# Chunked attention with a channel mix on one core: q and k of the first tiles loaded two tokens a partition, with a reordered start

## The chip, the cores and the metric

The kernel runs on one core of a Trainium2 chip. The metric is the device time of one execution in microseconds, as the median of several runs. The engines are TensorE (PE, with its weight loads PEld), VectorE (DVE), ScalarE (ACT), GpSimd (POOL) and SyncE (SP). SP issues nearly all DMAs, in the order in which the program names them; each engine works off its own instructions in order.

## The reference

q, k and v are (8, 8, 576, 64): batch, heads, tokens, head dimension, float32. The weights of the channel mix come in float64 and are read as words.

```python
# attention inside chunks of 64 tokens
scores = scale * q_c @ k_c^T          # per batch, head, chunk: 64 x 64
attn = softmax(scores)                # max subtracted, 1e-9 added to the sum
x = heads side by side of attn @ v_c  # (8, 576, 512)
# channel mix
x_prev = x shifted by one token, zero at the start of a batch
xk = mu_k * x + (1 - mu_k) * x_prev
xr = mu_r * x + (1 - mu_r) * x_prev
k = relu(xk @ w_k)                    # 512 -> 1024
v = (k * k) @ w_v                     # 1024 -> 512
out = sigmoid(xr @ w_r) * v
```

## The kernel before

The 8 x 576 = 4608 tokens are cut into 36 tiles of 128 tokens, two to a group of 256 (18 groups). A tile holds two chunks of 64 tokens. Its work is named by tasks:

- **n, b, v, s** are loads on SP: `nq`/`nk` q and k in natural layout (tokens on partitions) for the first six tiles, `bq`/`bk` 32 x 32 blocks of q and k for the later groups, `v`, and `swr`, `swk`, `swv` the staged pieces of 1 MB of the weights (two of w_r, four of w_k, four of w_v).
- **T** brings q and k into the layout with the head dimension on partitions (`qT`, `kT`, one buffer each): for the first six tiles by PE transposes (line 318) and copies out of PSUM (133), later by DVE's block transpose (339).
- **S** are the scores (363) and the softmax: maximum (373), subtraction (379), exp on ACT (383), sums (387 to 389), normalization (393). **P** transposes the probabilities (420), multiplies by v (438) and writes x.
- **Mk, Mr** are the two token mixes. For tiles 0 to 3 PE makes them by products with diagonal matrices of mu and 1 - mu (528); later tiles use DVE, with a difference d (510) and four operations of 128 columns (540). Each mix is split into a high and a low part, in the format of the fast products.
- **c, h** turn a staged float64 piece into a high and a low part, with two ACT operations (258, 262), two DVE operations (265, 271), a copy (133) on either engine and a subtraction on DVE (280).
- **K, R, V** are the products with w_k (580), w_r (629) and w_v (659), each in three passes of high and low parts. **K** is followed by relu (594), square (601) and the split (133, 613), **R** by the sigmoid (643), **V** by the product with it and the store (672, 674).

A staged w_k piece lies in a slot of a later w_v tile, the w_r pieces and the first two w_v pieces in rings of the K results, and the last two w_v pieces in one ring called `st`, of one buffer. The diagonals lie in that ring too (line 481). `d` and `mix` tiles have two buffers each.

The order of all instructions is written by hand. `START` lists every step of the first groups, with the engine behind a colon (A for ACT, D for DVE), as in

```python
W:14 Mk3.0:D nq0.0 nk0.0 T0.2 T0.0 T0.3:D mu.0:A T0.1:D Mk0.0:D nq1.0 P0.3:D nk1.0 T1.0 S0.0
```

`T0.2` is the third step of task T0, `W:14` fourteen warm-up products. `GROUP` lists the steps of one pass of the loop for groups 2 to 17, which computes K, R and V of its group, attention and mixes of the next, and the loads of the ones behind. Semaphores between the engines follow from the tiles that the steps read and write.

Of the kernel before, what the change touches and what calls it, by code (L numbers as in the profile page):

```python
# [7 lines left out]
F32 = mybir.dt.float32  # L8
# [3 lines left out]
AF = mybir.ActivationFunctionType  # L12
ALU = mybir.AluOpType
# [11 lines left out]


START = """
W:14 Mk3.0:D nq0.0 nk0.0 T0.2 T0.0 T0.3:D mu.0:A T0.1:D Mk0.0:D nq1.0 P0.3:D nk1.0 T1.0 S0.0
S0.1:D swr0.0 dg.0:A v0.0 S0.2:D nk2.0 S0.3:A T1.1:D T1.2 T1.3:A cwr0.0:A S1.0 nk3.0 cwr0.1:A
S0.4:D S0.5:D S1.1:D T2.2 S1.2:D T2.3:A nq2.0 cwr0.2:D P0.0 cwr0.3:D P0.1:A P0.2 swr1.0 S1.3:A  # L30
T3.2 P0.4:A nq3.0 S1.4:D S1.5:D hwr0.0:A cwr1.0:D Mr0.0 cwr1.1:A v1.0 T2.0 P1.0 swk0.0 hwr0.1:D
nq4.0 T2.1:A P1.1:A P1.3:D cwr1.2:D Mk0.1 nk4.0 T3.3:A cwr1.3:D Mr0.1:A S2.0 T3.0 S2.1:D P1.2
Mk0.2:A Mr0.2:D nq5.0 T3.1:A S2.2:D S3.0 P1.4:A nk5.0 T4.2 swk1.0 S3.1:D cwk0.1:A Mk0.3:D
cwk0.0:A S3.2:D S2.3:A T4.0 T4.3:A Mk1.1 hwr1.0:A v2.0 Mr1.0 swk3.0 T4.1:A Mk1.2:A T5.2 Mr1.1:A
S2.4:D S2.5:D T5.3:A hwr1.1:D Mk1.3:D S3.3:A swk2.0 cwk0.2:D cwk0.3:D cwk1.1:A Mr1.2:D P2.0
P2.1:A hwk0.0:A S3.4:D T5.0 S3.5:D P2.3:D Mk2.0:D Mk1.0:D hwk0.1:D R00.0 P2.2 R00.1:A R01.0
P2.4:A cwk2.1:A cwk1.0:D cwk1.2:D T5.1:A P3.0 cwk1.3:D P3.1:A cwk2.0:A Mr2.0 Mr2.1:A K00.0
hwk1.0:D v3.0 hwk1.1:D cwk2.2:D R01.1:A P3.2 cwk2.3:D cwk3.0:A S4.0 K01.0 S5.0 swv1.0 P3.3:D
Mk2.1 swv0.0 cwk3.1:A hwk2.0:A cwk3.2:D hwk2.1:D cwk3.3:D K00.1:A K01.1:A K02.0 K00.2:A
hwk3.0:D cwv0.0:A K01.2:A hwk3.1:D bq3.0 cwv0.1:A Mr2.2:D K03.0 P3.4:A cwv1.0:A Mk2.2:A  # L40
cwv0.2:D P4.3:D cwv0.3:D Mk3.1 Mk2.3:D v4.0 cwv1.1:A Mr3.0 swv2.0 Mk3.2:D Mk3.3:D S4.1:D
K00.3:A Mr3.1:A K00.4:D hwv0.0:A Mr3.2:D K02.1:A R10.0 K10.0 K01.3:A T6.0:D K02.2:A cwv1.2:D
K02.3:A K01.4:D cwv1.3:D R11.0 R10.1:A K03.1:A cwv2.0:A cwv2.1:A K11.0 hwv0.1:D K03.2:A K02.4:D
R11.1:A K03.3:A S5.1:D cwv2.2:D V001.0 cwv2.3:D K10.1:A K03.4:D hwv2.0:A hwv1.0:A S4.2:D S4.3:A
hwv2.1:D K12.0 V001.1 v5.0 hwv1.1:D V001.2 K10.2:A S5.2:D S4.4:D S5.3:A bk3.0 K11.1:A K11.2:A
K10.3:A S4.5:D S5.4:D K10.4:D swv3.0 P4.0 P4.1:A K11.3:A S5.5:D cwv3.1:A V001.3 P4.2 cwv3.0:D
K11.4:D K12.1:A K13.0 K12.2:A bq4.0 P4.4:A V001.4 cwv3.2:D cwv3.3:D hwv3.0:A P5.3:D P5.0 V001.5
T7.0:D P5.1:A K13.1:A hwv3.1:D V001.6 Mk4.0:D K12.3:A V001.7 Mk4.1:D V001.8:D Mk4.2:A P5.2 v6.0
V10.0 P5.4:A V001.9:D V10.1 V11.0 Mk5.0:D Mr4.0:D V11.1 K13.2:A K13.3:A Mr4.1:A Mk4.3:D K12.4:D
Mk5.1:D V10.2 V10.3 Mk5.2:A K13.4:D V11.2 V11.3 V10.4 Mr4.2:D Mk5.3:D V11.4 V10.5 V11.5 v7.0  # L50
T6.1:D V10.6 Mr5.0:D Mr5.1:D V10.7 V11.6 Mr5.2:D V11.7 bk4.0 T7.1:D V11.8:D V10.8:D
"""
# [26 lines left out]
def tile_chunk_attention_channel_mix(  # L79
# [57 lines left out]
    def queue(e):  # L137
        return nc.scalar if e == "A" else nc.sync
# [7 lines left out]
    def segments(first, many):  # L146

        cut = -first % S
        if 0 < cut < many:
            return [(0, cut), (cut, many - cut)]  # L150
        return [(0, many)]

    def load_nat(t):
        for nm, src in (("q", q), ("k", k)):
            do.task = f"n{nm}{t}"

            def fn(_, nm=nm, src=src):
                g, tl = divmod(t, 2)
                if tl == 0:
                    T[f"{nm}{g}"] = ld.tile([P, 2, HP, 2, D], F32, tag=nm, name=f"{nm}n_{g}")  # L160
                dst = T[f"{nm}{g}"]
                for s, n in segments(t * TT, TT):
                    b, t0 = divmod(t * TT + s, S)
                    for j in range(2):
                        nc.sync.dma_start(  # L165
                            out=dst[s : s + n, tl, :, j, :],
                            in_=src[b, j * HP : (j + 1) * HP, t0 : t0 + n, :].rearrange(
                                "h p d -> p h d"
                            ),
                        )  # L170
# [135 lines left out]
    kT = att.tile([P, HP, G], F32, name="kT", bufs=1)  # L306
    halves = [slice(j * CH, (j + 1) * CH) for j in range(2)]

    def move_qk(t):

        g, tl = divmod(t, 2)
        do.task = f"T{t}"
        for nm, to in (("q", qT), ("k", kT)):

            def f_tr(_, nm=nm):
                x = T[f"tr{nm}{t}"] = ps_k.tile([P, HP, TT], F32, tag="k", name=f"tr{nm}_{t}")
                for hp in range(HP):
                    nc.tensor.transpose(
                        out=x[:, hp, :],
                        in_=T[f"{nm}{g}"][:, tl, hp],  # L320
                        identity=ident,
                    )

            def f_move(e, nm=nm, to=to):
                copy(e, to[:, :, tl * TT : (tl + 1) * TT], T[f"tr{nm}{t}"])

            do(f_tr, "P")
            do(f_move, "A")

    def att_qk(t):  # L330

        g, tl = divmod(t, 2)
        tb = slice(tl * (TT // 32), (tl + 1) * (TT // 32))
        part = slice(tl * TT, (tl + 1) * TT)
        do.task = f"T{t}"
        for nm, to in (("q", qT), ("k", kT)):

            def f_move(_, nm=nm, to=to):
                nc.vector.transpose(
                    out=to[:, :, part].rearrange("p h (t i) -> p h t i", i=32),  # L340
                    in_=T[f"{nm}{g}"][:, :, tb, :],
                )

            do(f_move, "D")
# [132 lines left out]
    def make_diag():  # L477
        do.task = "dg"

        def fn(e):  # L480
            T["diag"] = tmp.tile([P, 4, NB, P], F32, tag="st", name="diag", bufs=1)
            for i, (nm, mu) in enumerate((("k", muk), ("r", mur))):
                rest = const.tile([P, NB], F32, name=f"rest{nm}")
                nc.vector.tensor_scalar(rest, mu, -1.0, 1.0, ALU.mult, ALU.add)
                for n, col in enumerate((mu, rest)):
                    to = diag[nm, n] = T["diag"][:, 2 * i + n]
                    for cb in range(NB):
                        if e == "A":
                            nc.scalar.activation(
                                to[:, cb], ident, AF.Copy, scale=col[:, cb : cb + 1]  # L490
                            )
# [187 lines left out]
    load_mu()  # L679
    make_diag()  # L680
    for t in range(6):
        load_nat(t)
        load_v(t)
    for f in range(4):
        convert_wk(f, slots[f])
# [10 lines left out]
            ("kk0", "kk1", "st", "st")[i],  # L696
        )
    for t in range(6):
        move_qk(t)
        att_scores(t)  # L700
        att_values(t)
        x_mix(t)
        if t in (1, 3):
            g = t // 2
            for fp in range(NF // 2):
                moe_k(g, fp)
            for tl in range(2):
                moe_r(g, tl)
# [86 lines left out]
```

## Time and profile before

| | us |
|---|---|
| median of the runs (3) | 617.93 |
| lowest, highest | 614.33, 619.47 |
| the profiled execution, device time | 620.49 |
| its span | 618.7 |

| engine | busy us (share of the span) |
|---|---|
| PE | 601.6 (97%) |
| PEld | 529.2 (86%) |
| DVE | 399.8 (65%) |
| ACT | 332.5 (54%) |
| POOL | 0.7 (0%) |

In the profile a line such as L580 is a line of the kernel; the names behind it are the tiles written and read, then partitions x elements, and a number of instructions. A float32 product that isn't a transpose appears as two matmul records. A row of the chain of waits has a start, a length and what the time went to. A row of a stretch of time has its bounds, its length, the busy time of PE, PEld, DVE, ACT and POOL with the number of instructions, the granted TensorE clock, the busy share of the DMA engines, and GB/s. A row of the timeline has start, length, engine, line, operation, tiles, and in square brackets the idle time before it and what ended it.

### The profile page before, as it was taken

How to read it: one execution, taken by the hardware profiler on the slowest of the kernel's cores; microseconds unless marked ns; L12 is line 12 of the kernel's file. 1: busy time of each engine (PE TensorE's matmuls, PEld its weight loads, DVE VectorE, ACT ScalarE, POOL GpSimd, SP SyncE). 2: the span in 40 equal slices, each digit the busy share in tenths (PEclk: the TensorE clock that was granted, in tenths of full speed). 3: DMA queues.
4: the chain of work that ended last, by engine and by line, in shares of the span. 5: the costliest groups of instructions: out<-in, count | busy, mean ns of one | idle time of the engine just before them, and what ended most of it. 6: DMA issues, size and time to landing. Idle time of an engine off the chain costs nothing.

```text
span 618.7 us, 14035 instructions
## 1 busy us (share of the span) xinstructions
PE 601.6 (97%) x5676; PEld 529.2 (86%) x5676; DVE 399.8 (65%) x860; ACT 332.5 (54%) x519; POOL 0.7 (0%) x6
## 2 busy tenths in 40 slices
PE   5888999999999999999999999999999999999997
PEld 5778988989898989888888888898989898989895
DVE  2767879757666667666666666666766667675610
ACT  4767684454545464646463737372728282827250
POOL 0000000000000000000000000000000000000000
PEclk9798999999999999999999999999999999999999
DMA  8796343244233434242322442234233334020000
GB/s 190 219 280 172 105 109 78 43 88 94 36 56 75 105 70 85 52 90 48 75 52 39 90 98 34 56 79 103 34 62 68 74 77 83 19 57 13 18 18 34
DMA packets 195071, 49.17 MB, mean 79 GB/s; under 512 B 186816, under 2 KB 186816, under 8 KB 195008
## 3 DMA queue, kind: packets, MB, share of 16 engines
q1 hardware_dynamic: 193952, 48.29, 34.9%
q8 instruction: 44, 0.72, 0.5%
q10 hardware_dynamic: 1056, 0.00, 0.1%
q14 instruction: 19, 0.16, 0.1%
HBM read 38.80 MB, written 9.44 MB: 78 GB/s over the span
## 4 chain that ended last, share of the span: by engine, by line
PE 91%; DMA 4%; SPq 3%; DVE 1%; issue 0%; ACT 0%; DVEq 0%
PE pk L580 33%; PE pv L659 33%; PE pr L629 16%; PE xps L438 3%; PE s L363 3%; DMA wk_st<-in_moe_w_k 3%; PE pt L420 2%; SPq L165 2%; SPq L182 1%; DMA wr_st<-in_moe_w_r 1%; PE mxk L528 1%; PE mxr L528 0%; SPq L254 0%; DVE wk_st L265 0%; DVE wk L280 0%
## 5 line engine op out<-in xcount | busy, mean ns | idle before, releaser
L580 PE MATMUL pk<-xkhi,wk 128*128 128x256 f32 x1152 | 217.9, 285 | 1.9 <-DVE wk L133 1.1
L659 PE MATMUL pv<-wv,kk 128*128 128x512 f32 x864 | 205.4, 395 | 0.0
L659 PEld LDWEIGHTS pv<-wv,kk 128*128 128x128 f32 x864 | 161.4, 187 | 39.2 <-DVE wv L280 0.2
L580 PEld LDWEIGHTS pk<-xkhi,wk 128*128 128x128 f32 x1152 | 181.3, 189 | 4.2 <-DVE wk L133 1.3
L580 PE MATMUL pk<-xklo,wk 128*128 128x256 f32 x576 | 162.3, 282 | 0.0
L580 PEld LDWEIGHTS pk<-xklo,wk 128*128 128x128 f32 x576 | 109.3, 190 | 0.9
L594 ACT ACTIVATE relu<-pk 128x512 f32<-128x512 f32 x72 | 42.6, 592 | 99.3 <-PE pk L580 99.3
L613 DVE TENSOR_TENSOR kk<-relu,kk 128x512 fp32r<-128x512 f32 x72 | 49.5, 687 | 69.9 <-ACT kk L131 69.9
L629 PE MATMUL pr<-wr,xrhi 128*128 128x512 f32 x288 | 93.7, 406 | 0.0
L629 PEld LDWEIGHTS pr<-wr,xrhi 128*128 128x128 f32 x288 | 51.4, 188 | 11.0
L629 PE MATMUL pr<-wr,xrlo 128*128 128x512 f32 x144 | 56.8, 395 | 0.0
L373 DVE TENSOR_REDUCE m<-s 128x8 f32<-128x512 f32 x36 | 24.7, 687 | 47.8 <-PE s L363 47.8
L131 ACT ACTIVATE xkhi<-mixk 128x512 fp32r<-128x512 f32 x32 | 20.2, 632 | 58.2 <-DVE mixk L540 58.2
L131 ACT ACTIVATE xrhi<-mixr 128x512 fp32r<-128x512 f32 x31 | 19.6, 632 | 57.0 <-DVE mixr L540 57.0
L131 ACT ACTIVATE kk<-relu 128x512 fp32r<-128x512 f32 x72 | 45.6, 633 | 2.1
L601 ACT ACTIVATE relu<-relu 128x512 f32<-128x512 f32 x72 | 45.5, 632 | 2.1
L540 DVE SCALAR_TENSOR_TENSOR mixk<-d,muk,x 128x128 f32<-128x128 f32 (+1 forms) x144 | 38.5, 332 | 1.0
L540 DVE SCALAR_TENSOR_TENSOR mixr<-d,mur,x 128x128 f32<-128x128 f32 (+1 forms) x144 | 38.3, 331 | 0.0
L559 DVE TENSOR_TENSOR xrlo<-mixr,xrhi 128x512 fp32r<-128x512 f32 x32 | 22.2, 692 | 21.0 <-ACT xrhi L131 21.0
L559 DVE TENSOR_TENSOR xklo<-mixk,xkhi 128x512 fp32r<-128x512 f32 x32 | 22.1, 692 | 20.9 <-ACT xkhi L131 20.9
L672 DVE TENSOR_TENSOR out<-pv,sg 128x512 f32<-128x512 f32 x36 | 24.0, 675 | 16.7 <-PE pv L659 15.7
L131 ACT ACTIVATE pT<-pt 128x512 f32<-128x512 f32 x36 | 21.3, 591 | 22.6 <-PE pt L420 22.6
(75 smaller groups left out, 562.9 us busy)
## 6 DMA issues: line engine op xcount, KB each, us to landing
v<-in_v SPq DMA_DIRECT2D x144, 64.0 KB, 2.5
out<-out SPq DMA_DIRECT2D x36, 256.0 KB, 2.2
q<-in_q SPq DMA_DIRECT2D x160, 32.0 KB, 2.0
k<-in_k SPq DMA_DIRECT2D x160, 32.0 KB, 2.0
wk_st<-in_moe_w_k SPq DMA_DIRECT2D x4, 1024.0 KB, 8.1
wv_st<-in_moe_w_v SPq DMA_DIRECT2D x4, 1024.0 KB, 7.2
wr_st<-in_moe_w_r SPq DMA_DIRECT2D x2, 1024.0 KB, 8.1
qn<-in_q SPq DMA_DIRECT2D x10, 128.0 KB, 2.9
```

Source lines behind the costliest of these rows:

```text
L131: nc.scalar.activation(to, x, AF.Copy)
L363: nc.tensor.matmul(scores()[halves[e], j, hp, :], qT[halves[j], hp, cols[e]], kT[halves[j], hp, cols[e]], start=True, stop=True,)
L373: nc.vector.tensor_reduce(out=heads(m), in_=scores(), axis=AX.X, op=ALU.max)
L540: nc.vector.scalar_tensor_tensor(out=m[:, cb, s : s + w], in0=d[:, cb, s : s + w], scalar=mu[:, cb : cb + 1], in1=x[:, cb, c : c + w], op0 ...
L559: engine[e].tensor_tensor(lo[:, :, part], T[f"m{nm}{t}"], hi[:, :, part].bitcast(F32), ALU.subtract)
L580: nc.tensor.matmul(pk[:, e, :], wk[a][:, cb, f * P : (f + 1) * P], xk[b][:, cb, :], start=(n == 0), stop=(n == 3 * NB - 1),)
L594: nc.scalar.activation(r, T[f"pk{g}{fp}"], AF.Relu)
L601: nc.scalar.activation(r, r, AF.Square)
L613: engine[e].tensor_tensor(lo, T[f"r{g}{fp}"], hi.bitcast(F32), ALU.subtract)
L629: nc.tensor.matmul(pr, xr[a][:, cb, tl * TT : (tl + 1) * TT], wr[b][:, cb, :], start=(n == 0), stop=(n == 3 * NB - 1),)
L659: nc.tensor.matmul(T[f"pv{g}{tl}"], kk[a][:, f, tl * TT : (tl + 1) * TT], wv[b, f // 4][:, f % 4, :], start=(f == 0 and n == 0), stop=(f = ...
L672: nc.vector.tensor_tensor(o, T[f"pv{g}{tl}"], T[f"sg{g}{tl}"], ALU.mult)
```

## The change

Five things change; the loop keeps all its operations.

- For the first six tiles q and k are loaded by group, two neighbouring tokens on a partition, eight heads in one DMA (two where a batch ends inside the group): 512 bytes in one piece instead of 256. A PE step then takes the tokens of one parity: for each pair of heads two ordinary products, each with 64 columns of q or k as stationary operand and the identity as moving operand, into one half of the PSUM partitions. Four such steps serve a group of two tiles. The copies out of PSUM write every second column of `qT` or `kT`.
- mu_k and mu_r are loaded as four rows each, turned by one PE transpose, and written by two ACT operations as mu and 1 - mu.
- The diagonals lie in the ring of the mix tiles, which has four buffers and serves `d` as well, and no longer in `st`. They are made by DVE, no longer by ACT.
- `START` has a new order throughout.
- In `GROUP`, Mr of the next group's first tile stands ahead of Mk of its second. (`T` tasks of the block transposes are called `D`.)

```diff
-W:14 Mk3.0:D nq0.0 nk0.0 T0.2 T0.0 T0.3:D mu.0:A T0.1:D Mk0.0:D nq1.0 P0.3:D nk1.0 T1.0 S0.0
-S0.1:D swr0.0 dg.0:A v0.0 S0.2:D nk2.0 S0.3:A T1.1:D T1.2 T1.3:A cwr0.0:A S1.0 nk3.0 cwr0.1:A
-...
+W:14 nq0.0 P0.3:D Mk0.0:D mu.0 nk0.0 swr1.0 mu.1 T0.0 mu.2:A T0.1:A T0.2 T0.3:A swr0.0 Mk3.0:D
+nq1.0 T0.6 dg.0:D T0.7:A T0.4 T0.5:A S0.0 S0.1:D S1.0 cwr1.0:A S0.2:D Mk1.0:D S0.3:A S1.1:D
+S1.2:D cwr1.1:A S1.3:A S0.4:D S0.5:D cwr0.1:A P0.0 T1.2 P0.1:A v0.0 cwr0.0:A S1.4:D T1.3:A T1.0
+nk1.0 P0.2 P0.4:A T1.1:A S1.5:D P1.0 v1.0 T1.4 T1.5:A P1.1:A Mr0.0 cwr1.2:D cwr1.3:D hwr1.0:A
+cwr0.2:D T1.6 cwr0.3:D Mr0.1:D P1.2 P1.3:D hwr0.0:A Mk0.1 swk0.0 T1.7:A Mr0.2:D hwr1.1:D S2.0
+nk2.0 P1.4:A nq2.0 Mk0.2:A hwr0.1:D Mk0.3:D S2.1:D S2.2:D cwk0.0:A swk2.0 cwk0.1:A S3.0
+cwk0.2:D Mk1.1 T2.4 cwk0.3:D T2.2 Mk1.2:A S2.3:A Mk1.3:D T2.3:A Mr1.0 T2.5:A S3.1:D swk3.0 T2.6
+swk1.0 P2.3:D S3.2:D hwk0.0:A cwk2.0:A Mr1.1:A v2.0 hwk0.1:D Mr1.2:D cwk2.1:A T2.7:A S2.4:D
+cwk3.1:A S2.5:D cwk3.0:A R00.0 cwk2.2:D cwk2.3:D K00.0 swv2.0 hwk2.0:D P2.0 hwk2.1:D K00.1:A
+R01.0 S3.3:A P2.1:A P2.2 S3.4:D cwk3.2:D cwk3.3:D Mk2.0:D S3.5:D cwk1.1:A R00.1:A T2.0 K00.2:D
+...

-K3.0 Pb.0 Pb.1 K3.1234 Tc R0 Pa.2 Pb.2 Pa.34 Pb.34 Lv Lk Mka R1 Mkb Mra Mrb Td V0 V1
+K3.0 Pb.0 Pb.1 K3.1234 Dc R0 Pa.2 Pb.2 Pa.34 Pb.34 Lv Lk Mka R1 Mra Mkb Mrb Dd V0 V1

 def load_nat(g):
+    dst = T[f"{nm}{g}"] = ld.tile([P, H, 2, D], F32, tag=nm, name=f"{nm}n_{g}")
+    for s, n in segments(g * G, G):
+        b, t0 = divmod(g * G + s, S)
+        nc.sync.dma_start(
+            out=dst[s // 2 : (s + n) // 2, :, :, :],
+            in_=src[b, :, t0 : t0 + n, :].rearrange("h (p r) d -> p h r d", r=2),
+        )

 def load_mu():
+    for i, mu in enumerate((mu_k, mu_r)):
+        queue(e).dma_start(out=mus[i * NB : (i + 1) * NB], in_=mu.rearrange("(c p) -> c p", p=P))
+    nc.tensor.transpose(out=T["mu"], in_=mus, identity=ident[: 2 * NB, : 2 * NB])
+    nc.scalar.activation(mu2[:, 0], x, AF.Copy)
+    nc.scalar.activation(mu2[:, 1], x, AF.Copy, scale=-1.0, bias=1.0)

 def move_qk(g):
+    x = T[f"tr{nm}{r}{g}"] = ps_k.tile([P, HP, P], F32, tag="k", name=f"tr{nm}{r}_{g}")
+    for hp in range(HP):
+        for j in range(2):
+            nc.tensor.matmul(
+                x[halves[j], hp, :],
+                T[f"{nm}{g}"][:, j * HP + hp, r, :],
+                ident,
+                start=True,
+                stop=True,
+            )
+    copy(e, to.rearrange("p h (c r) -> p h r c", r=2)[:, :, r, :], T[f"tr{nm}{r}{g}"])

 def make_diag():
-    T["diag"] = tmp.tile([P, 4, NB, P], F32, tag="st", name="diag", bufs=1)
+    to = diag[nm, n] = mo.tile([P, NB, P], F32, tag="mix", name=f"diag_{nm}{n}", bufs=4)

 def x_mix(t):
-    d = T[f"d{t}"] = mo.tile([P, NB, TT], F32, tag="d", name=f"d_{t}", bufs=2)
+    d = T[f"d{t}"] = mo.tile([P, NB, TT], F32, tag="mix", name=f"d_{t}", bufs=4)
-    m = T[f"m{nm}{t}"] = mo.tile([P, NB, TT], F32, tag="mix", name=f"mix{nm}_{t}")
+    m = T[f"m{nm}{t}"] = mo.tile([P, NB, TT], F32, tag="mix", name=f"mix{nm}_{t}", bufs=4)
```

More of the change, by code (lines that the diff above doesn't have):

```diff
@@ L27 @@
 START = """
-W:14 Mk3.0:D nq0.0 nk0.0 T0.2 T0.0 T0.3:D mu.0:A T0.1:D Mk0.0:D nq1.0 P0.3:D nk1.0 T1.0 S0.0
-S0.1:D swr0.0 dg.0:A v0.0 S0.2:D nk2.0 S0.3:A T1.1:D T1.2 T1.3:A cwr0.0:A S1.0 nk3.0 cwr0.1:A
[L30 to L51, printed above, removed]
+W:14 nq0.0 P0.3:D Mk0.0:D mu.0 nk0.0 swr1.0 mu.1 T0.0 mu.2:A T0.1:A T0.2 T0.3:A swr0.0 Mk3.0:D
@@ new lines @@
+swk1.0 P2.3:D S3.2:D hwk0.0:A cwk2.0:A Mr1.1:A v2.0 hwk0.1:D Mr1.2:D cwk2.1:A T2.7:A S2.4:D
+cwk3.1:A S2.5:D cwk3.0:A R00.0 cwk2.2:D cwk2.3:D K00.0 swv2.0 hwk2.0:D P2.0 hwk2.1:D K00.1:A
+R01.0 S3.3:A P2.1:A P2.2 S3.4:D cwk3.2:D cwk3.3:D Mk2.0:D S3.5:D cwk1.1:A R00.1:A T2.0 K00.2:D
+T2.1:A P2.4:A R01.1:A hwk3.0:A hwk3.1:D cwk1.0:A K02.0 Mr2.0 Mk2.1 cwk1.2:D swv1.0 P3.0 Mr2.1:A
+cwk1.3:D K02.1:A hwk1.0:D swv0.0 P3.1:A hwk1.1:D K03.0 v3.0 S4.0 P3.3:D v4.0 P3.2 Mr2.2:D
+cwv2.1:A K01.0 cwv2.0:A cwv2.2:D K02.2:A P3.4:A cwv2.3:D bq3.0 cwv0.1:A Mr3.0 S4.1:D K00.3:A
@@ new lines @@
+Mk2.2:A P4.3:D Mk2.3:D cwv1.1:A K00.4:D Mr3.1:A K02.3:A Mr3.2:D hwv2.0:A S5.0 Mk3.1 S5.1:D
+Mk3.2:D cwv0.0:A K03.1:A K02.4:D K03.2:A R11.0 v5.0 Mk3.3:D R10.0 K01.1:A R11.1:A hwv2.1:D
+S5.2:D cwv1.0:A cwv0.2:D K10.0 swv3.0 cwv0.3:D K03.3:D K01.2:A R10.1:A K01.3:A K03.4:D K12.0
+S4.2:D hwv0.0:A K10.1:A hwv0.1:D cwv1.2:D cwv1.3:D S4.3:A bk3.0 K01.4:D cwv3.1:A hwv1.0:A
+K10.2:A K11.0 S5.3:A S4.4:D V001.0 K10.3:A hwv1.1:D S4.5:D S5.4:D V001.1 P4.0 V001.2 cwv3.0:A
+V001.3 cwv3.2:D P4.1:A V001.4 K12.1:A P4.2 cwv3.3:D K12.2:A hwv3.0:A D7.1:D S5.5:D V001.5 P5.0
@@ L52 @@
+hwv3.1:D K10.4:D V001.6 K12.3:A K12.4:D V001.7 P4.4:A Mk4.0:D K13.0 Mr4.0:D P5.1:A K11.1:A
+P5.3:D V001.8:D D6.0:D P5.2 K11.2:A K11.3:A V001.9:D K13.1:A bk4.0 V11.0 P5.4:A V10.0 K11.4:D
+V11.1 K13.2:A K13.3:A V11.2 Mk4.1:D V10.1 K13.4:D V10.2 Mk5.0:D Mk4.2:D Mk5.1:D V10.3 bq4.0
+V10.4 V11.3 D7.0:D Mk5.2:D v6.0 Mr4.1:A Mk4.3:D V11.4 V10.5 Mr4.2:D V10.6 V11.5 Mk5.3:D D6.1:D
+Mr5.0:D V11.6 Mr5.1:D V11.7 V10.7 V10.8:D v7.0 Mr5.2:D V11.8:D
 """
@@ L125, in tile_chunk_attention_channel_mix @@
     make_identity(nc, ident)
-    muk = const.tile([P, NB], F32, name="muk")
-    mur = const.tile([P, NB], F32, name="mur")
+    mus = const.tile([2 * NB, P], F32, name="mus")
+    mu2 = const.tile([P, 2, 2, NB], F32, name="mu2")
+    muk, mur = mu2[:, 0, 0], mu2[:, 0, 1]
     def copy(e, to, x):
@@ L151, in segments, with load_nat @@
         return [(0, many)]
-    def load_nat(t):
+    def load_nat(g):
         for nm, src in (("q", q), ("k", k)):
-            do.task = f"n{nm}{t}"
+            do.task = f"n{nm}{g}"
             def fn(_, nm=nm, src=src):
[L158 to L170, printed above, removed]
+                dst = T[f"{nm}{g}"] = ld.tile([P, H, 2, D], F32, tag=nm, name=f"{nm}n_{g}")
[5 more added lines that the diff above has]
+                    )
             do(fn, "Q")
@@ L215, in fn, with f_tr, f_move @@
         def fn(e):
-            queue(e).dma_start(out=muk, in_=mu_k.rearrange("(c p) -> p c", p=P))
-            queue(e).dma_start(out=mur, in_=mu_r.rearrange("(c p) -> p c", p=P))
-        do(fn, "Q")
+            for i, mu in enumerate((mu_k, mu_r)):
+                queue(e).dma_start(
+                    out=mus[i * NB : (i + 1) * NB], in_=mu.rearrange("(c p) -> c p", p=P)
+                )
+        def f_tr(_):
+            T["mu"] = ps_k.tile([P, 2 * NB], F32, tag="k", name="mu_t")
+            nc.tensor.transpose(out=T["mu"], in_=mus, identity=ident[: 2 * NB, : 2 * NB])
+        def f_move(e):
+            x = T["mu"].rearrange("p (i c) -> p i c", i=2)
+            nc.scalar.activation(mu2[:, 0], x, AF.Copy)
+            nc.scalar.activation(mu2[:, 1], x, AF.Copy, scale=-1.0, bias=1.0)
+        do(fn, "A")
+        do(f_tr, "P")
+        do(f_move, "A")
     wk = [wts.tile([P, NB, FF], F32R, name=f"wk{s}") for s in range(2)]
@@ L307, in tile_chunk_attention_channel_mix, with move_qk, f_tr, f_move @@
     halves = [slice(j * CH, (j + 1) * CH) for j in range(2)]
-    def move_qk(t):
-        g, tl = divmod(t, 2)
-        do.task = f"T{t}"
+    def move_qk(g):
+        do.task = f"T{g}"
         for nm, to in (("q", qT), ("k", kT)):
[L315 to L328, printed above, removed]
+            for r in range(2):
+                def f_tr(_, nm=nm, r=r):
+                    x = T[f"tr{nm}{r}{g}"] = ps_k.tile([P, HP, P], F32, tag="k", name=f"tr{nm}{r}_{g}")
[7 more added lines that the diff above has]
+                                stop=True,
+                            )
+                def f_move(e, nm=nm, to=to, r=r):
+                    copy(e, to.rearrange("p h (c r) -> p h r c", r=2)[:, :, r, :], T[f"tr{nm}{r}{g}"])
+                do(f_tr, "P")
+                do(f_move, "A")
     def att_qk(t):
@@ L334, in att_qk @@
         part = slice(tl * TT, (tl + 1) * TT)
-        do.task = f"T{t}"
+        do.task = f"D{t}"
         for nm, to in (("q", qT), ("k", kT)):
@@ L480, in fn @@
         def fn(e):
-            T["diag"] = tmp.tile([P, 4, NB, P], F32, tag="st", name="diag", bufs=1)
[L482 to L486, printed above, removed]
+            for i, nm in enumerate("kr"):
+                for n in range(2):
+                    to = diag[nm, n] = mo.tile([P, NB, P], F32, tag="mix", name=f"diag_{nm}{n}", bufs=4)
                     for cb in range(NB):
+                        col = mu2[:, n, i, cb : cb + 1]
                         if e == "A":
-                            nc.scalar.activation(
-                                to[:, cb], ident, AF.Copy, scale=col[:, cb : cb + 1]
-                            )
-                        else:
-                            nc.vector.tensor_scalar(
-                                to[:, cb], ident, col[:, cb : cb + 1], None, ALU.mult
-                            )
+                            nc.scalar.activation(to[:, cb], ident, AF.Copy, scale=col)
+                        else:
+                            nc.vector.tensor_scalar(to[:, cb], ident, col, None, ALU.mult)
         do(fn, "D")
@@ L681, in tile_chunk_attention_channel_mix @@
     for t in range(6):
-        load_nat(t)
+        if t % 2 == 0:
+            load_nat(t // 2)
         load_v(t)
@@ L698, in tile_chunk_attention_channel_mix @@
     for t in range(6):
-        move_qk(t)
+        if t % 2 == 0:
+            move_qk(t // 2)
         att_scores(t)
```

## The prediction

> **What bounds the kernel now.** I read the busy shares, then the chain that ended last, then both cut by stage.
>
> ```profile
> span 618.7 us, 14035 instructions
> ...
> PE 601.6 (97%) x5676; PEld 529.2 (86%) x5676; DVE 399.8 (65%) x860; ACT 332.5 (54%) x519; POOL 0.7 (0%) x6
> ```
> ```profile
> 54.27 4.28 PE pk L580 x22
> ...
> 112.33 2.84 PE pk L580 x24
> ...
> 143.95 2.84 PE pk L580 x24
> ```
> ```profile
> 0.00:54.27 54.27, 41.05 (x510) 36.56 (x510) 31.94 (x51) 37.09 (x60) 0.70 (x6) 0.90 0.89 237
> 54.27:112.33 58.06, 58.06 (x440) 51.53 (x441) 49.36 (x86) 36.77 (x54) 0.00 (x0) 0.97 0.39 91
> 112.33:143.95 31.62, 31.62 (x306) 27.77 (x306) 21.45 (x47) 15.46 (x25) 0.00 (x0) 1.00 0.33 67
> ```
>
> ```profile
> 134.71 1.14 DVE L540 SCALAR_TENSOR_TENSOR mixk<-d,muk,x 128x128 f32<-128x128 f32 x4
> ...
> 136.55 0.69 DVE L559 TENSOR_TENSOR xklo<-mixk,xkhi 128x512 fp32r<-128x512 f32 x1 [0.70 <-ACT xkhi L131]
> ```
>
> The windows fence gives length, busy time of PE, PE's weight loads, DVE, ACT and POOL, the granted clock, the DMA share and GB/s. From 54.27 us on PE never waits. The groups of the steady loop (from 112.33) are PE at full clock, 31.62 us each, with DVE at 21.45 and ACT at 15.46. There the diff only moves Mr of the first tile ahead of Mk of the second and makes the d and mix tiles share four buffers; Mk of the second tile, done at 137.2 now, ends later on DVE by a mix (1.14), its copy and its low part, 2.5 us, and the next group's K product (143.95) still comes 4 us after that. So the loop keeps its length, and everything is decided in the hand-ordered start, which ends at 112.33.
>
> **Where the start loses time.** Up to 54.27 PE is busy 41.05 us, 5.9 of them the warm-up. The chain shows DMA and its issue:
>
> ```profile
> 5.07 8.26 DMA wr_st<-in_moe_w_r
> ...
> 36.70 10.81 DMA wk_st<-in_moe_w_k
> ```
> ```profile
> 5.07 0.51 SPq L254 DMA_DIRECT2D wr_st<-in_moe_w_r  x1
> ...
> 10.31 2.82 SPq L165 DMA_DIRECT2D kn<-in_k  x1
> 13.35 0.37 SPq L165 DMA_DIRECT2D kn<-in_k  x1
> ```
> ```profile
> 2.00:7.00 5.00, 5.00 (x29) 5.00 (x28) 0.00 (x0) 2.56 (x5) 0.00 (x0) 1.00 1.10 214
> 12.00:13.00 1.00, 0.00 (x0) 0.00 (x0) 0.00 (x0) 1.00 (x5) 0.00 (x0) 1.00 0.23 55
> ...
> 42.00:44.00 2.00, 2.00 (x39) 1.66 (x36) 1.14 (x1) 1.98 (x2) 0.00 (x0) 1.00 1.05 406
> ```
> ```profile
> 47.53 1.14 ACT L262 ACTIVATE wk_st<-wk_st 128x1024 int32<-128x1024 uint32 x1 [2.30 <-DMA wk_st<-in_moe_w_k]
> ```
>
> Between the wr load (5.07) and the k load at 13.35 lie seven issues; the eighth goes out when wr has landed (5.07 + 8.26 = 13.33). So eight loads are in flight at most, a 1 MB load holds up the eighth behind it, and the engines run dry (55 GB/s in the microsecond from 12). With 28 issues for q and k of the first six tiles, in 256-byte pieces (214 GB/s, against 406 for the 4 KB rows of the weights), the quarter of w_k that is loaded last is waited for until 47.53.
>
> The second loss is PE's:
>
> ```profile
> 1.05 5.86 PE L723 MATMUL warm<-idle 128*128 128x128 f32 x28 [1.05 <-DVE idle L121]
> ...
> 10.29 1.28 ACT L489 ACTIVATE diag<-ident,restk 128x128 f32<-128x128 f32 x4 [4.27 <-DVE restk L484]
> ...
> 13.82 0.61 ACT L383 ACTIVATE p<-p 128x512 f32<-128x512 f32 x1
> 14.34 0.57 ACT L131 ACTIVATE kT<-trk 128x512 f32<-128x512 f32 x1
> 14.81 1.13 ACT L258 ACTIVATE wr_st<-wr_st 128x1024 f32<-128x1024 f32 x1
> 14.96 1.13 PE L363 MATMUL s<-kT,qT 64*64 64x64 f32 x32 [4.95 <-ACT kT L131]
> 17.79 1.09 PE L420 MATMUL pt<-ident,p 128*128 128x128 f32 x4 [0.65 <-DVE p L379]
> ```
> ```profile
> 19.87:23.30 3.43, 3.43 (x45) 3.24 (x38) 2.81 (x6) 2.22 (x4) 0.00 (x0) 0.50 0.61 143
> 40.35:43.78 3.43, 1.95 (x38) 1.65 (x39) 1.29 (x3) 3.41 (x4) 0.00 (x0) 1.00 1.06 379
> 50.60:54.00 3.40, 1.66 (x66) 1.32 (x66) 3.30 (x4) 3.40 (x6) 0.00 (x0) 1.00 0.88 212
> 54.00:57.43 3.43, 3.16 (x15) 3.16 (x15) 3.40 (x5) 1.60 (x2) 0.00 (x0) 0.51 0.29 47
> ```
>
> Twelve diagonal blocks stand on ACT ahead of the first exp and of a k move; the scores wait 4.95 us for that move, and PE's clock is at half until 23.30, and again from 54.00.
>
> **The change part by part.** Prices first:
>
> ```profile
> 58.56 0.62 PE s L363 x32
> ...
> 66.84 1.78 PE mxk L528 x16
> ...
> 70.41 2.84 PE pr L629 x12
> 73.25 2.84 PE pk L580 x24
> ...
> 90.60 0.62 PE xps L438 x32
> ...
> 95.67 0.44 PE pt L420 x4
> ...
> 115.17 1.09 PE s L363 x64
> ```
> ```profile
> 9.49 0.69 DVE L373 TENSOR_REDUCE m<-s 128x8 f32<-128x512 f32 x1 [0.80 <-PE s L363]
> ...
> 15.18 0.17 DVE L388 TENSOR_SCALAR z<-z 128x8 f32<-128x8 f32 x1
> ...
> 17.56 1.22 DVE L265 SCALAR_TENSOR_TENSOR wr_st<-wr_st 128x1024 int32<-128x1024 int32 x1
> ```
>
> *Turning by half-array products.* A transpose is one record of 0.11 us (pt: four in 0.44). The new ones are ordinary f32 products with the identity as moving operand, two records each of 0.11 us like mxk (16 in 1.78), eight products a step. One after the other a step is 1.78 us; with both halves of the array side by side, 0.89. No row shows half-array products. The nearest are the quarter-array scores: 32 records of half the moving columns would be 1.78 in a row and take 0.55 (64 in 1.09), 3.3 times as fast out of 4. The same share of 2 gives 1.09. I take 1.0 a step, bounds 0.89 to 1.78. Twelve steps (three groups, q and k, two parities) are 12.0 us; now six tiles have q and k at 0.44, 5.3. PE's work grows by 6.7 us. The Trainium skill (TensorEngine Tiling (Array Packing), Key Properties) says that a change of tiling mode drains the array, which speaks against this part. The trace has a pair of such changes at 0.62 - 1.09/2 = 0.07 us, and by that ten more pairs would add 0.7 us, an estimate that lies inside the 1.0.
>
> *Loads.* q and k go from 28 issues to 8, in 512-byte pieces (between 214 and 406 GB/s; the sum needs only the lower end). Eight in flight now hold some 5 MB, so no issue before w_k's last quarter stands behind an unlanded weight for long. Up to w_k's first quarter the bytes are as before, 5.8 MB: 2.6 MB at 214 and 3.15 MB at 406, from 2 us on, is 22 us; its last quarter is in by 22 + 4.9 + 7.8 = 35. ACT comes to them at 29 and 44 in the walk below: DMA leaves the path.
>
> *mu by rows* removes 1,024 four-byte pieces and adds one small PE transpose behind the warm-up and two small ACT moves: nothing, unless ACT's table load (1.28) waits for them; the last T0 move is still set by PE then. *Diagonals on DVE*: 16 at 0.29 (134.71) is 4.6 us at most, from 7.6 to 12.2; DVE's first work otherwise is tile 0's maximum at 12.3. Bounds 0 to 1.4 late. ACT loses 5.1 us. Without "st" held by the diagonals the third w_v load no longer waits for mxr; its next, swv3, waits on SP for that conversion (68), with bk3, bk4, bq4 behind it; bk3's 16 issues then land by 78, wanted at 85.
>
> *The new order, walked by hand*, each queue in order. Warm-up ends 6.9. Four T0 steps of 1.0, and the last move (0.6): scores 0 and 1 from 11.65 to 12.85 (now the second begins at 14.96). Softmax 0: 1.45 maximum and subtract, 1.3 for tile 1's same two in between (covering the exp), 1.2 for the sums (0.69, two ops on eight columns as at 15.18, and the gaps), 0.7 norm: P0 at 16.95. T1, whose data are there, is queued behind P0 on PE, so PE idles 4.1 us, 0.9 less than the 4.95 now. Its clock then halves for about a window and a half, 5.1 us, costing 2.6. From there PE has T1, P0, P1, the mixes of tiles 0 and 1, T2 and R00 without a wait: R00 at 36.4, K00 39.2 to 42.0.
>
> Sum: PE's work now is 58.06 less 1.6 for the half clock, plus 28.5 before 54.27 (T 5.3, four scores 2.4, three P 3.2, five mixes 8.9, two R 5.6, K00 3.1): 85.0. New end of the start = 6.9 + 85.0 + 6.7 + 0.7 (last T0 move) + 4.1 + 2.6 + 1.5 for small waits (bounds 0 to 7.6, below) = **107.5**, against 112.33: **4.8 us less**, 615.7 for the profiled execution (620.49, 1.8 outside its span). That execution was 2.6 above the median of the runs, 617.93, so the median goes to **613.0**.
>
> **The rivals.** *DVE becomes the bound.* Between 26.9 and the low half of w_k's last quarter it has 14 ops of 1.23, ten of 0.65, two of half that (casts) and 2.5 of small ones, 27.6 us: 54.5, wanted by K01 at 58. Such slack of some 3 us holds up to the last w_v part (86.6 against 89.5). With DVE filled at 85% as in 54.27 to 112.33, 59.7 us of work take 70.2 and PE waits 7.6; but that fill was set by PE. Halfway, with 3.8 in place of the 1.5, the gain is 2.5: 615.4; at the full price the kernel is 1.3 slower, 619.2.
>
> *The clock stays full.* By the windows it halved after one in which PE was busy 1.66 of 3.40 and stayed after 1.95 of 3.43; 4.1 us of idling split over two windows leaves 40%, so it should halve. If it does not, 2.6 us more are gained: 610.4. The Trainium skill (TensorE: Matmul & The Clock Gate, The HAM clock gate) says that the clock falls after a whole idle window of about 3.4 us, which 4.1 us seldom hold, so by it this rival would be the likelier. The trace disagrees: the clock halved at 54.00 after a window with 1.66 us of work in it.
>
> *The halves do not overlap.* A step is then 1.78: 12 x 0.78 = 9.4 us, and 1 more at the half clock. It decides from 1.4 us a step on, where the gain is used up; here it ends 5.6 us slower, 623.5. Against it speaks that quarter-array products overlap in the trace.
>
> **How the numbers follow.** Forecast 45% (its own range 610 to 615), DVE 30%, clock 14%, halves 11%. A measurement of this kernel tells about 1% (6.2 us) from no change. Faster by over 1% (below 611.8): the clock case and 20 of the forecast's 45, 34%; slower (above 624.1): half of the last case, 6%; the rest 60%. The range from 608 to 619 takes in the full price on DVE and the clock case, with 2 us below for steps at their 0.89 bound, and leaves out the halves.
>
> **What would show it.** K00 at 39 to 43 us; no microsecond of DMA under 100 GB/s before 30 us; T steps of 16 records in 1.0 us (1.78 is the slow rival); P0 near 17 with PE's clock at half behind it; PE waits for wk or wv low halves on DVE (the DVE rival); the loop's 31.62 unchanged. A start ending after 110 or before 104, or a changed loop, would make the prediction wrong.

## The result, and the profile after

The changed kernel is slower. Its median is 634.62 us (630.5 to 635.06) against 618.4 us (the kernel before, now with six executions), a ratio of 1.0258 with an interval of 1.0219 to 1.0297. The forecast was 613.0, with a range of 608 to 619. The profiled execution took 634.7 us, 632.8 of them its span.

First the head of its page:

```profile
span 632.8 us, 14294 instructions
...
PE 613.7 (97%) x5821; PEld 539.0 (85%) x5821; DVE 403.0 (64%) x876; ACT 327.6 (52%) x503; POOL 0.7 (0%) x6
```

The chain of waits, with the K products at which each pass of the loop begins after the first:

```profile
45.97 2.84 PE pk L586 x24
...
158.24 2.83 PE pk L586 x24
...
189.85 2.84 PE pk L586 x24
```

The loop's period is 31.61 us (189.85 - 158.24); it was 31.62. But its second pass begins at 158.24 and not at 143.95: 14.3 us later, which is the difference of the two spans (14.1). The first pass begins at 113.80, by the first row below, and not at 112.33. So 1.5 us are lost in the start, and 12.8 inside the first pass. PE's timeline, its queue of waits and the stretches of time show where:

```profile
113.80 0.28 PE L586 MATMUL pk<-xkhi,wk 128*128 128x256 f32 x1
...
135.36 0.47 PE L450 MATMUL xps<-pT,v 64*64 64x64 f32 x2 [5.06 <-DMA v<-in_v]
```
```profile
PE xps L450 <- DMA v<-in_v: 6.7, 7, 5.1
```
```profile
7.20:43.00 35.80, 28.17 (x442) 25.08 (x442) 24.80 (x47) 21.37 (x31) 0.00 (x0) 0.86 1.08 311
43.00:111.50 68.50, 68.50 (x615) 60.85 (x616) 58.54 (x102) 46.19 (x66) 0.00 (x0) 1.00 0.28 66
111.50:130.00 18.50, 18.50 (x191) 17.23 (x189) 10.24 (x21) 9.62 (x17) 0.00 (x0) 1.00 0.21 33
130.00:146.00 16.00, 9.18 (x76) 6.62 (x75) 4.84 (x13) 3.56 (x5) 0.00 (x0) 0.60 0.41 94
```

From 43 us to 130 PE never waits. Then it waits for v of tiles 6 and 7, works at a mean clock of 0.60, and is busy 9.18 us of 16. The waits are 6.7 of the 12.8 us; the other 6, by subtraction, are what the lower clock adds to the work. SP's own queue tells why v is late (a start, the time that the issues took, and what was loaded; `bk3` is the load of k's blocks for group 3, `v6` that of v for tile 6, `V001` the product with w_v of both tiles of group 0):

```profile
75.61 9.96 SPq L198 DMA_DIRECT2D k<-in_k  x16
99.15 1.56 SPq L680 DMA_DIRECT2D out<-out  x2
100.77 16.14 SPq L198 DMA_DIRECT2D k<-in_k  x32
116.95 15.98 SPq L198 DMA_DIRECT2D q<-in_q  x32
133.02 2.59 SPq L177 DMA_DIRECT2D v<-in_v  x4
...
136.36 2.59 SPq L177 DMA_DIRECT2D v<-in_v  x4
```
```profile
SPq L680 <- DVE out L678: 14.2, 2, 13.5
```

After bk3 SP idles 13.5 us at the first store, which waits for V001's product. Behind the two stores stand bk4 and bq4, 64 issues of half a microsecond each, and behind these v6 and v7. PE wants v6 at 130.3; it lands after 135. In the kernel before bq4 stood ahead of the stores and bk4 behind v7, as its queue shows:

```profile
83.45 18.98 SPq L203 DMA_DIRECT2D q<-in_q  x34
...
103.03 2.60 SPq L182 DMA_DIRECT2D v<-in_v  x4
...
109.01 17.58 SPq L203 DMA_DIRECT2D k<-in_k  x32
```

In the start itself the queue of PE's waits shows two that the prediction didn't have, the second scores of a pair:

```profile
PE pt L432 <- DVE p L405: 4.0, 1, 4.0
PE s L375 <- DVE p L391: 2.1, 1, 2.1
...
PE s L375 <- DVE m L385: 0.8, 1, 0.8
```

and the chain shows what the longer one led to, a mix at half clock (3.36 us in place of 1.98):

```profile
31.74 0.69 DVE xklo L565
...
33.06 0.70 DVE p L391
...
33.80 0.89 PE s L375 x32
34.70 3.36 PE mxk L534 x16
```

### The profile page after: what moved, and what is told of

Its sections match the earlier page's. It is cut to its first block, busy times and chain, and to the rows that moved or that the text cites. A ratio compares the mean times of both kernels' runs of the same rounds, so it can differ in the third digit from the quotient of the medians.

```text
span 632.8 us, 14294 instructions
## 1 busy us (share of the span) xinstructions
PE 613.7 (97%) x5821; PEld 539.0 (85%) x5821; DVE 403.0 (64%) x876; ACT 327.6 (52%) x503; POOL 0.7 (0%) x6
## 4 chain that ended last, share of the span: by engine, by line
PE 91%; SPq 5%; DVE 1%; issue 1%; DMA 0%; ACT 0%; DVEq 0%
PE pk L586 31%; PE pv L665 30%; PE pr L635 16%; SPq L198 5%; PE xps L450 3%; PE s L375 3%; PE pt L432 2%; PE mxk L534 1%; PE mxr L534 1%; PE trq L328 1%; PE warm L731 1%; PE trk L328 1%; SPq L177 1%; DMA v<-in_v 0%; DVE p L391 0%
## 5 line engine op out<-in xcount | busy, mean ns | idle before, releaser
L635 PE MATMUL pr<-wr,xrhi 128*128 128x512 f32 x288 | 95.4, 413 | 0.0
L546 DVE SCALAR_TENSOR_TENSOR mixk<-d,mu,x 128x128 f32<-128x128 f32 (+1 forms) x144 | 38.5, 332 | 1.0
L546 DVE SCALAR_TENSOR_TENSOR mixr<-d,mu,x 128x128 f32<-128x128 f32 (+1 forms) x144 | 38.3, 330 | 0.0
```

The source lines that it names most:

```text
L546: nc.vector.scalar_tensor_tensor(out=m[:, cb, s : s + w], in0=d[:, cb, s : s + w], scalar=mu[:, cb : cb + 1], in1=x[:, cb, c : c + w], op0 ...
L635: nc.tensor.matmul(pr, xr[a][:, cb, tl * TT : (tl + 1) * TT], wr[b][:, cb, :], start=(n == 0), stop=(n == 3 * NB - 1),)
```

## The experiments

Each ratio is to executions of the kernel before that were made beside the run, with medians from 617.35 to 618.4; where two runs were not made together, their ratios compare better than their medians. The last column is read from the one profiled execution of a run.

| run | median us | ratio to before, interval | loop begins at |
|---|---|---|---|
| the kernel before, profiled twice | 617.35 to 618.4 | | 112.33; 110.48 |
| the changed kernel | 634.62 | 1.0258, 1.0219 to 1.0297 | 113.80 |
| loads first | 620.96 | 1.0048, 1.0027 to 1.0068 | 112.67 |
| only v first | 622.26 | 1.0062, 1.0033 to 1.009 | 113.26 |
| before, with late blocks | 629.76 | 1.02, 1.0153 to 1.0248 | 111.98 |
| loads first, scores in pairs | 616.62 | 0.9987, 0.9968 to 1.0005 | 108.38 |
| + full-array transposes (other columns) | 609.91 | 0.988, 0.9849 to 0.991 | 101.66 |
| + T1 in the gap (half-array) | 614.43 | 0.995, 0.9928 to 0.9973 | 105.43 |
| + 256-byte pieces, 16 issues | 617.26 | 0.9999, 0.9975 to 1.0023 | 109.19 |
| + loads and turning as before | 617.11 | 0.998, 0.9958 to 1.0001 | 109.31 |
| + the same, T1 in the gap | 617.03 | 0.9982, 0.9966 to 0.9998 | 108.84 |

**Loads first.** Theory: SP's queue is the whole of the loss in the first pass.

```diff
 hwv3.1:D K10.4:D V001.6 K12.3:A K12.4:D V001.7 P4.4:A Mk4.0:D K13.0 Mr4.0:D P5.1:A K11.1:A
-P5.3:D V001.8:D ... V001.9:D K13.1:A bk4.0 ... V10.3 bq4.0 ... v6.0 ... V10.8:D v7.0
+P5.3:D bk4.0 v6.0 V001.8:D ... V001.9:D v7.0 K13.1:A ... V10.3 bq4.0 ... V10.8:D
```

> The changed kernel; in the start's order only three load steps move: bk4 and v6 stand ahead of the first store (V001.8), v7 right behind the second store, bq4 keeps its place. Theory (SP's queue): bk4 waits behind two stores until 100.8 us and bk4 and bq4 then take 32 issues each ahead of v6 and v7, so that PE waits 5.1 us and more for v and loses its clock; with v ahead the PE wait at 130 us is gone, the loop's first K product stays at 113.8, and the time falls by 12 to 13 us to 621 to 623. Rival (the blocks are late anyway): bq4 stays behind the stores, DVE's transposes of tile 8 wait for it, and the time stays at 628 to 634.

620.96 us, 13.7 less than the changed kernel. PE no longer waits for v, and the second pass begins one period after the first:

```profile
112.67 2.84 PE pk L586 x24
...
144.30 2.84 PE pk L586 x24
```

**Only v first.** v6 and v7 ahead of bk4, all four behind the two stores.

```diff
-V001.9:D K13.1:A bk4.0 ... bq4.0 ... v6.0 ... v7.0
+V001.9:D K13.1:A v6.0 v7.0 bk4.0 ... bq4.0 ...
```

> The changed kernel; only v6 and v7 move ahead of bk4, the two stores stay ahead of all of them. Theory (SP's queue): v6 and v7 are issued from 101 to 106 us and PE's wait for v is gone; bk4 and bq4 then end at 138 instead of 133, so DVE's transposes of tile 8, which come at 130.7 in its queue, wait some 8 us, and the mixes behind them are late for the next K product by a few us: 622 to 628. Rival (it is the stores' wait of 13.5 us and not the order of the loads): 634.

622.26 us. The waits of DVE (in total, times, longest) show the block transposes late, by 2.1 us and not by 8:

```profile
DVE qT L351 <- DMA q<-in_q: 2.1, 1, 2.1
```

PE does not wait for them in the first pass. The queue stays late for some passes, and at 243.7 us one wait of PE, 0.5 us for `kT`, comes of it. So the 13.5 us that SP idles at the store cost little by themselves (1.3 us between the medians of these two runs, 0.6 of them in the start, where the two kernels are alike); the 64 block issues ahead of v are the loss.

**Before, with late blocks.** The kernel before with `bk4.0 bq4.0 v6.0` in this order behind V001.9.

```diff
-... bq4.0 ... V001.8:D ... v6.0 ... V001.9:D ... v7.0 ... bk4.0 ...
+... V001.8:D ... V001.9:D bk4.0 bq4.0 v6.0 ... v7.0 ...
```

> The kernel before, with the load order of the changed one at the end of its start: bk4, bq4, v6 behind the two stores of V001, in that order. Theory (SP's queue): the stores leave at 102 to 106 us, 64 issues of 0.48 us follow, v6 goes out at some 138 and lands at 140, wanted at 128.7; PE waits 11 to 14 us in the first pass of the loop, and the kernel before slows to 629 to 633. Rival (the loss comes from the new start, not from the queue): 618.

629.76 us: 12.2 us slower than before (617.53 beside it), with nothing else of the change in it. PE waits for v as in the changed kernel, here in the slowest of the four executions (633.35 us), and the first pass takes 44.8 us (from 111.98 to 156.81) in place of 31.62:

```profile
PE xps L438 <- DMA v<-in_v: 8.3, 5, 7.3
```

**Scores in pairs.** On top of the loads first, both scores of a group are written before the first is read.

```diff
-S0.0 S0.1:D S1.0 cwr1.0:A S0.2:D
+S0.0 S1.0 S0.1:D cwr1.0:A S0.2:D
-S2.0 ... hwr0.1:D Mk0.3:D S2.1:D S2.2:D cwk0.0:A swk2.0 cwk0.1:A S3.0
+S2.0 ... hwr0.1:D Mk0.3:D S3.0 S2.1:D S2.2:D cwk0.0:A swk2.0 cwk0.1:A
```

> As the first run (bk4, v6 and v7 earlier), and S1.0 stands ahead of S0.1, S3.0 ahead of S2.1, so that the scores of two tiles, which share one PSUM tile, are both written before the first is read. Theory (a wait that the prediction missed): PE's waits for DVE at the second scores (0.8 us at 13.3, 2.1 us at 33.8) go, the clock stays full from 34 to 38, and K00 comes 4 to 5 us earlier (41 instead of 46): 3 to 5 us less than the first run, 617 to 619. Rival (DVE sets the pace of the start): the waits move to K00 or K02 for the low parts of w_k, and the time is that of the first run.

616.62 us, 4.3 less. Both waits are gone from PE's queue; the first softmax is left:

```profile
PE pt L432 <- DVE p L405: 4.7, 1, 4.7
...
PE s L375 <- ACT kT L132: 0.7, 1, 0.7
```

and the chain has K00 and the first K product of the loop:

```profile
40.39 2.84 PE pk L586 x24
...
108.38 2.84 PE pk L586 x24
```

K00 comes at 40.39 where the walk had 39.2, and the loop begins at 108.38 where the sum had 107.5. Part of this closeness is luck: the warm-up ended at 6.17 here and not at the walk's 6.9.

**Full-array transposes.** The same kernel, with four transposes of other columns in place of the eight products of a step. Heads come to wrong places by it, so that its time stands for the work alone.

```diff
-for hp in range(HP):
-    for j in range(2):
-        nc.tensor.matmul(x[halves[j], hp, :], T[f"{nm}{g}"][:, j * HP + hp, r, :], ident, ...)
+for hp in range(HP):
+    nc.tensor.transpose(out=x[:, hp, :], in_=T[f"{nm}{g}"][:, 2 * hp + r], identity=ident)
```

> As the run with the scores in pairs, but each T step is four transposes of the full array (one record each) in place of eight half-array products (two records each). It turns other columns than the reference wants, so heads go to wrong places: its time stands for the work only. Theory (PE sets the pace from 17 us on, and the half-array products are dear): a step falls from 0.95 to 0.44 us at full clock, twelve steps give 6.1 us, of which the first four also bring the first softmax forward: 5 to 7 us less than the run with pairs, 610 to 612. Rival (DVE and the w_k conversions set the pace): PE gets waits at K00 to K01 instead, 0 to 3 us less.

609.91 us, 6.7 less than the run with pairs, and the loop begins 6.7 earlier (101.66). The half-array products' price lies on the path in full, and PE still names no low part of a weight among its waits.

**T1 in the gap.** `T1.2 T1.0` ahead of `P0.0`, in the run with pairs.

```diff
-cwr0.1:A P0.0 T1.2 P0.1:A v0.0 cwr0.0:A S1.4:D T1.3:A T1.0
+cwr0.1:A T1.2 T1.0 P0.0 P0.1:A v0.0 cwr0.0:A S1.4:D T1.3:A
```

> As the run with the scores in pairs, and the two q steps of T1 stand ahead of P0.0 on PE, in the 4.7 us in which PE waits for the first softmax. Theory (PE sets the pace): their 3.6 us at half clock leave the path and PE's clock falls later or not at all, 2.5 to 4 us less than the run with pairs: 612.5 to 614. Rival (nq1 has not landed by 12 us, 3.7 MB at 380 GB/s and 2 us of latency): the steps wait for the load, P0 is late by up to 1 us, and the time is the same or 1 us longer.

614.43 us, 2.2 less than the run with pairs (2.5 to 4 were expected) and 0.5% less than before (ratio 0.995, 0.9928 to 0.9973): the fastest complete version here. The profiled execution is the fastest of its ten, 613.43 us. In it PE's waits are cut into short ones (first fence), and the clock stays full through them (second fence):

```profile
PE trq L328 <- DMA qn<-in_q: 1.8, 1, 1.8
...
PE pt L432 <- DVE p L405: 0.9, 1, 0.9
```
```profile
12.00:16.00 4.00, 2.10 (x43) 1.75 (x32) 3.63 (x7) 2.35 (x4) 0.00 (x0) 1.00 1.25 261
16.00:20.00 4.00, 2.13 (x44) 1.62 (x46) 3.85 (x7) 3.37 (x5) 0.00 (x0) 1.00 0.84 222
```

Not every execution keeps it: five of the ten have a mean granted clock of 1.000 and take 613.43 to 615.07 us; the slowest, 617.29 us, has 0.991.

**256-byte pieces.** The run with pairs, with one DMA for each parity.

```diff
-nc.sync.dma_start(out=dst[s // 2 : (s + n) // 2, :, :, :], in_=src[...].rearrange("h (p r) d -> p h r d", r=2))
+for r in range(2):
+    nc.sync.dma_start(out=dst[s // 2 : (s + n) // 2, :, r, :], in_=src[...].rearrange("h (p r) d -> p h r d", r=2)[:, :, r])
```

> As the run with the scores in pairs, but q and k of the first six tiles are loaded in pieces of 256 bytes, one DMA for each parity (16 issues, not 8). Theory (DMA has left the path): the last quarter of w_k lands some 3 to 5 us later than now and still ahead of ACT's use of it; no change, within 1 us. Rival (the 512-byte pieces carry the start): the first scores and the w_k conversions wait, 3 to 6 us longer.

617.26 us against 616.62. Here, where the half-array products hold PE back, pieces of half the size in twice the issues cost 0.6 us.

**The kernel before again.**

> The kernel before, unchanged, for a second profile: the first one was of an execution of 620.49 us, 2.6 above the median. Theory: what an execution has above the lowest lies in the start, where the clock is halved for other stretches from run to run; the loop and the tail take 506.4 us from 112.33 to the end, as before. An execution at 617 would begin the loop at 109. Rival: the loop itself varies.

618.07 us; its profiled execution took 618.64, with a span of 616.8. Its loop begins at 110.48, by this row of its chain:

```profile
110.48 2.84 PE pk L580 x24
```

From there to the end are 616.8 - 110.48 = 506.3 us; from 112.33 to 618.7 they were 506.4, and in the run with pairs 614.6 - 108.38 = 506.2. So all that differs between these executions lies in the start. By this a median of 617.5 (with 1.8 outside the span) begins its loop at 109.4.

**Loads and turning as before.** The run with pairs, with the old 28 issues and full-array transposes of the right columns: all the rest of the change stays.

```diff
-dst = ... ld.tile([P, H, 2, D], ...)          # one DMA for a group
+dst = ... ld.tile([P, 2, HP, 2, D], ...)      # per tile and half of the heads, as before
-nc.tensor.matmul(x[halves[j], hp, :], T[f"{nm}{g}"][:, j * HP + hp, r, :], ident, ...)
+nc.tensor.transpose(out=x[:, hp, :], in_=T[f"{nm}{g}"][:, r, hp], identity=ident)
-copy(e, to.rearrange("p h (c r) -> p h r c", r=2)[:, :, r, :], ...)
+copy(e, to[:, :, r * TT : (r + 1) * TT], ...)
```

> As the run with the scores in pairs, with loads and turning as before the change: q and k in 256-byte pieces, 28 issues, four full-array transposes a step, plain copies. The new order, mu, the diagonals' place and the moved loads stay. Theory (the half-array products are dear by 6.7 us, the loads in pieces of 512 bytes worth nothing): 609.5 to 611.5, as with the wrong columns plus at most 1 us for the loads. Rival (with 28 issues SP and its eight loads in flight hold the weights up again): PE waits for nk1 or for low parts of w_k, 613 to 618.

The rival's time is right: 617.11 us, 7.2 more than with transposes of other columns (0.998 against 0.988 of the kernel before, by which it is 6.2). The chain of this run and the waits of PE:

```profile
22.05 6.66 DMA wk_st<-in_moe_w_k
28.73 1.04 SPq L165
...
31.77 2.81 DMA qn<-in_q
...
34.68 0.75 PE trq L332 x4
```
```profile
PE trq L332 <- DMA qn<-in_q: 3.0, 1, 3.0
PE trk L332 <- DMA kn<-in_k: 2.4, 2, 1.2
```

The first w_k piece, issued at 22.05, lands at 28.71, and the eighth load behind it goes out at 28.73: the same mechanism as in the kernel before, now with q of group 2 behind it, on which PE waits until 34.68. The rival had named nk1 or low parts of w_k; the waits are for q and k of group 2 (3.0 and 1.2 us) and for k of the first group (1.2), and the mix behind them runs at half clock, 3.30 us.

**The same, T1 in the gap.**

> As the run just named, with the two q steps of T1 ahead of P0.0. The loads of nq1 (four issues, after nq0, nk0 and w_r) land no earlier than with one issue, where PE waited 1.8 us for them. Theory: the two steps are only 0.9 us of work now and their half-clock share goes, 0.5 to 2 us less than the run just named: 608 to 610.5. Rival: nq1 is later still and P0 waits behind it, 0 to 2 us more: 610 to 613.

617.03 us, the same as the run just named (617.11), and so nearer to the rival; both ranges started from a base some 6 to 8 us too low. With four issues nq1 lands so late that PE waits 5.3 us for it, and the gap isn't used; the other 1.9 us of the row are for q of group 2.

```profile
PE trq L332 <- DMA qn<-in_q: 7.2, 2, 5.3
```

## Why the prediction was wrong, step by step

**The queue behind swv3 (the step that failed, 12.8 us).** The paragraph on mu and the diagonals followed SP's queue past swv3 only as far as bk3 ("wanted at 85") and named bk4 and bq4 behind it without working out when v6 and v7 go out; the sum has no term for it, and took the loop to keep its length from its first pass on. It also left out the stores: they are issued inside the V steps and stand in the same queue, and bk4 had moved behind two of them. From rows of before it could have been worked out: 32 block issues took 17.6 us there, so 64 take some 35, from the stores at 102.5 and 105.7 on, against v wanted at 128.7:

```profile
128.66 1.09 PE xps L438 x64
```

In the changed kernel they took 32 us from 100.8 on, and v6 went out at 133.02. Even the part that was worked out ran late: bk3's issues ended at 85.6 and were forecast to land by 78. Loads first takes away 13.7 us, v alone moved ahead 12.4, and the late blocks alone put 12.2 us into the kernel before.

**"From there PE has T1, P0, P1, the mixes ... without a wait" (failed, 4.3 us).** The scores of two tiles share one PSUM tile, and in the new order the second is written after the first has been read. The profile of before had this wait:

```profile
PE s L363 <- DVE p L379: 0.9, 1, 0.9
```

The walk left it out at both places, and the 1.5 us that the sum has for small waits did not cover it. At S3 it took 2.1 us, since the subtraction stood behind a low part that waited for ACT, and the clock halved after it. With the scores in pairs, 4.3 us less, K00 and the loop come within 1.2 us of the walk.

**From the profiled execution to the median (failed, about 3 us).** The sum of 4.8 us was made against an execution that began its loop at 112.33, and then taken off a median whose loop, by the second profile, begins at some 109.4. Against that the sum's 107.5 was worth 1.9 us, 615.6. The run with pairs, 108.38 and 616.62, bears this out: 4.1 us less than the first profile of before in span, but 0.9 less between medians.

**Half-array products (right).** A step of 1.0 was forecast; two in a row took 0.95 each, one by itself 1.02:

```profile
7.34 1.90 PE trq L328 x32
...
52.67 1.02 PE trq L328 x16
```

Both halves run side by side (one after the other a step would be 1.78), and the extra 6.7 us were on the path: 6.7 by the experiment with full transposes. The rival of halves that don't overlap is refuted, though the kernel is slower. One reading was off without harm: the price of a pair of mode changes, 0.62 - 1.09/2 = 0.07, is too small by half, since the row of 64 records holds a pair too. If a row is its work plus one pair, 1.09 - 0.62 = 0.47 is the work of 32 records and 0.15 the pair; the steps above give 1.90 - 1.02 = 0.88 and 0.14 in the same way.

**Loads (right that DMA leaves the path, not that it comes free).** No PE wait and no ACT wait before 60 us names a load in the changed kernel. With full-array transposes 28 issues in 256-byte pieces cost 7.2 us against eight in 512-byte pieces (6.2 by the ratios); with half-array products 16 issues in 256-byte pieces cost 0.6. This speaks for the number of issues and not the size of the pieces, but no run has the one without the other, nor 28 issues with half-array products. As far as these runs go the two parts of the change cancel: eight loads save 6 to 7 us, and the products which their layout needs cost 6.7.

**DVE as the bound (refuted).** No PE wait names a low part of w_k or w_v, in the changed kernel or in the faster ones made from it. (The operations that the prediction lists for DVE add up to 26.9 us and not 27.6, which decides nothing.) Making the diagonals on DVE took 0.21 us each and hid before the first maximum.

**The clock (right).** It was forecast to halve behind the softmax; it did, to means of 0.66 and 0.50 in these windows:

```profile
16.00:19.40 3.40, 1.39 (x8) 1.09 (x10) 3.19 (x9) 2.25 (x4) 0.00 (x0) 0.66 0.84 183
19.40:22.80 3.40, 3.40 (x36) 3.07 (x36) 3.37 (x4) 2.08 (x3) 0.00 (x0) 0.50 1.10 314
```

**The loop's order and shared buffers (right).** The period stayed at 31.61. mu by rows was not tried by itself; its PE step takes 0.22 us ahead of T0, and no wait of PE names it.

## What to carry to other kernels

When an order is rewritten, write down the whole queue of each issuing engine, stores included, with a time for every issue, as far as the last load that the next stage wants: a transfer that is cheap to move is held by everything that it is moved past. Small loads in a row cost places in the queue as well as bytes: where only so many may be in flight (here eight), one large load holds up the small one that many places behind it. And a gain worked out on one profiled execution counts from that execution; before it is taken off a median, a second profile shows how much of the loss was that execution's own.

## What the hardware showed that was not expected

The clock fell without a whole idle window in front of it. In the kernel before it halved at 54.00, after 3.40 us with 1.66 of work. In the changed kernel it halved in front of the mix at 34.70, where no wait of PE is longer than 2.1 us:

```profile
30.00:33.50 3.50, 1.70 (x42) 1.44 (x40) 2.89 (x5) 2.39 (x3) 0.00 (x0) 1.00 1.05 389
33.50:37.00 3.50, 3.19 (x43) 3.08 (x44) 2.70 (x3) 0.21 (x1) 0.00 (x0) 0.59 1.17 285
```

The Trainium skill (TensorE: Matmul & The Clock Gate, The HAM clock gate) names a whole idle window as the condition; these runs have the fall without one. With T1 in the gap, where one wait of 4.7 us is cut into several of under 2, the clock stayed full through 2.10 and 2.13 us of work in 4.00. How much work keeps it full is not shown: between 12.20 and 15.60 that execution worked only 1.62 of 3.40 us and kept its clock, and where the clock's own windows begin is not in the trace.

The same 28 warm-up records took 5.86 us in the first profile of the kernel before, 4.99 in its second and 6.14 in the changed kernel, and in the other runs from 4.79 to 6.31:

```profile
1.05 4.99 PE L723 MATMUL warm<-idle 128*128 128x128 f32 x28 [1.05 <-DVE idle L121]
```
```profile
1.05 6.14 PE L731 MATMUL warm<-idle 128*128 128x128 f32 x28 [1.05 <-DVE idle L121]
```

All the work behind them in the start shifts with that, so that the point at which the loop begins, read from one profile each, compares two runs to no better than 1 or 2 us. Of the 1.85 us between the two profiles of the kernel before, 0.87 lie in the warm-up. That this and the places at which the clock halves are what separates executions of one kernel, by up to 6 us, is argued and not shown: where in time the clock's windows fall was not controlled in any run.
